# The walk of the sums of the complex products: channel innermost in place of frequency innermost

## The chip, the cores and the metric

The kernel runs on one core of one Trainium2 chip. The metric is the device time in microseconds (us) of one execution; a kernel's time is the median of its runs. Engines: PE is TensorE (PEld its weight loads), DVE is VectorE, ACT is ScalarE, POOL is GpSimd, SP is SyncE, which issues most of the transfers.

## The reference, cut to what matters

Two blocks follow each other on a sequence of S = 2048 rows and D = 640 channels: a long convolution that is gated, and a token-mixing network of two matrix products. The change lies in the long convolution:

```python
kv = k_shift * v                                   # short convolution of k, times v
kv_f = rfft(kv padded to 2 * S along the sequence)
kf_f = rfft(ssm_k padded to 2 * S)
y_f = kv_f * kf_f                                  # complex, per channel
y = irfft(y_f)[:S] + kv * ssm_D
x = x + ga * (h * y)                               # h: the normalized, modulated input
```

After it come a second normalization, `gelu(h @ w1 + b1) @ w2 + b2` along the sequence, a gate and the residual. A complex product is four real products and two sums: the real part is a difference, the imaginary part a sum. These two sums are what the change touches.

## The kernel before, in words

The channels go through the convolution in five blocks of 128 (`c` = 0 to 4; the texts call them blocks 0 to 4). A partition holds a position of the sequence or of the spectrum for half of the channels, and the transform is split in two steps of matmuls on PE in each direction:

- `step1(side, t)` (line 218) is the first step of the forward transform, for the data (`side` 0) and for the filter (`side` 1). ACT copies its result from PSUM to Z (line 220).
- `f2(g)` (line 234) is the second step, for group g of 8 frequencies, eight groups a block. Its result lies in PSUM, data and filter side by side. ACT copies the filter's part to `kt` (line 238). `mul` then makes the products on DVE, two instructions of 512 elements a partition, into one of two halves of the tile P (`pa` and `pb`, 512 words each). `add` makes the two sums from P into Y, 256 elements a partition each.
- `i2(r)` (line 263) is the first step back. It reads Y as the weights of its matmuls, all 64 frequencies of two channels at a time, so it needs the sums of all eight groups. ACT copies its result to `T2` in the tile of Z (line 271; in the last block half of it on DVE, line 269).
- `i1(half)` (line 282) is the second step back, into PSUM.
- `gate` multiplies by the normalized input on DVE and adds to the residual on POOL (the tiles xa and xb).

All elementwise operations of two tensors go through one helper, `TT`, and so all show line 59 in the profile; their tiles tell them apart: p is written by `mul`, y by `add`, tap, kt and x by the short convolution, aux by the gate and the modulation.

The order of work is written out by hand, each engine takes its instructions in that order, and the waits follow from the tiles. In the loop over the groups (`for g in range(8)`), the pass for g issues f2(g), the products of group g - 1, and the sums of group g - 2, and beside these, on ACT, two rows of the normalized input (line 289), and on DVE some operations of the next block's short convolution (`dv`). The sums go to POOL; only group 7's, in blocks 1 to 4, go to DVE (`pa_next(dve if c else pool)`). P has two halves, so the products of group g wait until the sums of group g - 2 have read them. After the loop PE takes two parts of the next block's `step1`, in blocks 1 to 3, and then `i2(0)`. In block 0 the modulation comes in between: SP loads the weights `w_mod` (line 335) and PE multiplies them (`mod_part`, line 342). `perm_add` is a small sum on POOL (one partition, 64 elements, in place with a step of 32 words) that adds `ssm_D` to the filter.

P and Y are laid out so: P holds for each of the 8 frequencies k, then for the two terms r, 32 channels i in a run; Y holds for real and imaginary part, for each of 32 channels, 64 frequencies in a run.

Of the kernel before, what the change touches and what calls it, by code (L numbers as in the profile page):

```python
# [49 lines left out]
def mixer_kernel(ctx: ExitStack, tc: tile.TileContext, q, k, v, shift_k, ssm_k, ssm_D, w1, b1, w2, b2, c,  # L50
# [8 lines left out]
    TT = lambda eng, o, a, b, op: eng.tensor_tensor(o, a, b, op=op)  # L59
    uid = [0]  # L60

    def mem(tag, n, name=None):

        return sb.tile([128, n], F32, name=name or tag, tag=tag, bufs=1)
# [4 lines left out]
    def psum(slot=None):  # L69

        uid[0] += 1
        slot = ring[uid[0] % len(ring)] if slot is None else slot
        return psp.tile([128, 1024], F32, name=f"pst_{uid[0]}", tag=f"pst{slot}", bufs=1)
# [23 lines left out]
    Y = T_y.rearrange("p (r i k) -> p r i k", r=2, i=32)  # L97
# [126 lines left out]
    def f2(g):  # L224

        ps = psum()
        for kk in range(8):
            k1 = 8 * g + kk
            for ri in range(2):
                for h in range(2):  # L230
                    o = 128 * kk + 64 * ri
                    rhs = bass.AP(tensor=T_z.tensor, offset=T_z.offset + 128 * h + 2 * k1,
                                  ap=[T_z.ap[0], [256, 32], [1, 2]])
                    pe.matmul(ps[64 * h:64 * h + 64, o:o + 64], W2[k1 // 32][:, 2 * (k1 % 32) + ri], rhs, start=True, stop=True)  # L234
        pv = ps.rearrange("p (m s i) -> p m s i", s=2, i=32)
        xs_ = pv[:, :, 0]
        kt = KT[g % 2]
        act.activation(kt.rearrange("p (m i) -> p m i", i=32), pv[:, :, 1], AF.Copy)  # L238
        pa, pb = P[:, 1024 * (g % 2):1024 * (g % 2) + 512], P[:, 1024 * (g % 2) + 512:1024 * (g % 2) + 1024]
        m16 = lambda t: t.rearrange("p (m i) -> p m i", i=32)  # L240

        def mul():
            TT(dve, m16(pa), xs_, m16(kt), ALU.mult)
            sw = bass.AP(tensor=kt.tensor, offset=kt.offset + 32, ap=[kt.ap[0], [64, 8], [-32, 2], [1, 32]])
            TT(dve, pb.rearrange("p (k r i) -> p k r i", k=8, r=2), xs_.rearrange("p (k r) i -> p k r i", r=2), sw,
               ALU.mult)

        def add(eng=pool):
            for ri, t, op in ((0, pa, ALU.subtract), (1, pb, ALU.add)):
                t = t.rearrange("p (k r i) -> p r i k", k=8, r=2)  # L250
                TT(eng, Y[:, ri, :, 8 * g:8 * g + 8], t[:, 0], t[:, 1], op)
        return mul, add


# [255 lines left out]
    for c in range(NC):  # L510
# [86 lines left out]
        else:  # L597
# [6 lines left out]
            t = mem("in", 4288, "wb3")  # L604
# [4 lines left out]
        if c:  # L609
            dv(7 if cn is not None else 8)  # L610
            i2(0)
            if cn is None:
                mod_part(tap, 3, pl[3])
                i2(1, dve)
                t = mem("y", 4096, "wb2")
# [390 lines left out]
    for s in range(NW):  # L1006
        i = NF + s
# [77 lines left out]
```

## Time and profile before

| | |
|---|---|
| median of 3 runs | 722.91 us (722.14 to 728.45) |
| span of the profiled execution | 727.4 us, granted clock 0.969 |
| PE busy | 656.2 us, 90% |
| DVE busy | 492.5 us, 68% |
| ACT busy | 297.3 us, 41% |
| POOL busy | 155.7 us, 21% |
| the sums on POOL | 72, 92.2 us in all |
| the sums on DVE | 8, 9.1 us in all |

The profile gives the span of the profiled execution, from its first instruction to its last, as its own time; it stands 4.5 us above the median of the runs. A row of a timeline or of the chain begins with the start in us from the span's start and the duration in us. A row that groups instructions ends with their total busy time in us, the mean of one in ns, and the idle time ahead of them on their engine with what ended it. `out<-in` are tile names; 128x512 is partitions by elements.

### The profile page before, as it was taken

The numbers are of one execution on the slowest core, as the hardware profiler recorded it, in microseconds if no ns is written. First come the engines' busy times: TensorE is split into PE (matmuls) and PEld (weight loads), VectorE is DVE, ScalarE is ACT, GpSimd is POOL, SyncE is SP. The second block draws the span as 40 slices with busy tenths as digits, with TensorE's granted clock in tenths as the row PEclk, the third lists the DMA queues.
The fourth block names the chain that finished last, engine by engine and source line by source line (L and its number), as shares of the span: only waits on it lengthen the run. The fifth ranks groups of instructions, "written<-read, shape, count | busy, mean of one in ns | idle before, by whom it ended". The sixth has DMA issues, their size and how long they took to land.

```text
span 727.4 us, 20779 instructions
## 1 busy us (share of the span) xinstructions
PE 656.2 (90%) x9131; PEld 632.1 (87%) x9131; DVE 492.5 (68%) x861; ACT 297.3 (41%) x465; POOL 155.7 (21%) x135
## 2 busy tenths in 40 slices
PE   0798868989999989987899999999999989999997
PEld 0798558988989989777799999999999989999997
DVE  7768458958879738678895312311299868888887
ACT  0533464535645645344776312311335222333222
POOL 5197029714725428100000000000000000000000
PEclk9999989989999999679999999999999999999999
DMA  9978988427243522333022353344163333455510
GB/s 184 242 223 221 388 147 169 112 45 166 45 80 87 169 54 69 110 88 88 10 50 58 62 113 60 59 93 81 50 188 102 116 104 117 149 156 174 150 53 37
DMA packets 167184, 84.90 MB, mean 117 GB/s; under 512 B 89235, under 2 KB 157622, under 8 KB 167094
## 3 DMA queue, kind: packets, MB, share of 16 engines
q1 hardware_dynamic: 162546, 82.27, 44.8%
q10 hardware_dynamic: 4548, 1.31, 1.0%
q8 instruction: 71, 1.16, 0.7%
q14 instruction: 19, 0.16, 0.1%
HBM read 73.07 MB, written 10.49 MB: 115 GB/s over the span
## 4 chain that ended last, share of the span: by engine, by line
PE 44%; DVE 24%; POOL 8%; SPq 7%; issue 6%; ACT 6%; DMA 5%; ACTq 0%; DVEq 0%; POOLq 0%
PE pst L432 21%; PE pst L1026 7%; POOL y L59 6%; PE pst L263 5%; DVE m_w L59 4%; PE pst L218 3%; SPq L495 3%; PE pst L282 3%; DVE m_x L59 3%; DVE tap L59 3%; PE pst L234 2%; ACT m_w L939 2%; DVE kt L59 2%; PE pst L951 2%; DMA in<-in_A_k_dram 2%
## 5 line engine op out<-in xcount | busy, mean ns | idle before, releaser
L234 PEld LDWEIGHTS pst<-z,w 128*64 128x64 f32 x2560 | 94.7, 141 | 7.7 <-ACT z L220 7.3
L234 PE MATMUL pst<-z,w 128*64 128x64 f32 x2560 | 95.7, 240 | 6.2 <-ACT z L220 6.1
L59 POOL TENSOR_TENSOR y<-p 128x256 f32<-128x256 f32 x72 | 92.2, 1340 | 22.3 <-DVE p L59 21.9
L59 DVE TENSOR_TENSOR p<-pst,kt 128x512 f32<-128x512 f32 x80 | 52.9, 689 | 24.8 <-ACT kt L238 14.3
L218 PE MATMUL pst<-v,x 128*64 128x128 f32 x640 | 46.3, 306 | 25.9 <-DVE x L59 25.9
L218 PEld LDWEIGHTS pst<-v,x 128*64 128x64 f32 x640 | 44.3, 221 | 26.5 <-POOL t L457 23.6
L220 ACT ACTIVATE z<-pst 128x1024 f32<-128x1024 f32 x40 | 45.8, 1146 | 52.1 <-PE pst L218 31.7
L263 PEld LDWEIGHTS pst<-v,y 32*128 32x128 f32 x1280 | 43.3, 210 | 6.7 <-POOL y L59 3.2
L263 PE MATMUL pst<-v,y 32*128 32x64 f32 x1280 | 45.4, 297 | 3.0 <-DVE y L59 2.1
L238 ACT ACTIVATE kt<-pst 128x512 f32<-128x512 f32 x40 | 25.1, 629 | 52.5 <-PE pst L234 30.2
L830 ACT ACTIVATE pst<-pst,sm 128x640 f32<-128x640 f32 x14 | 10.7, 767 | 85.9 <-PE pst L432 85.9
L951 PE MATMUL pst<-r_z,m_w 128*128 128x320 f32 x222 | 43.1, 313 | 3.0 <-DVE m_w L59 2.5
L218 PE MATMUL pst<-v,p 128*64 128x128 f32 x640 | 39.1, 281 | 4.8 <-DVE aux L59 3.2
L218 PEld LDWEIGHTS pst<-v,p 128*64 128x64 f32 x640 | 36.6, 141 | 6.0 <-DVE aux L59 3.5
L939 ACT ACTIVATE m_w<-m_v 128x896 fp32r<-128x896 f32 x24 | 22.1, 949 | 42.7 <-DVE m_v L59 31.0
L951 PEld LDWEIGHTS pst<-r_z,m_w 128*128 128x128 f32 x222 | 34.8, 188 | 5.0 <-DVE m_w L59 4.0
L59 DVE TENSOR_TENSOR tap<-tap,kt 128x512 f32<-128x512 f32 x51 | 35.6, 697 | 1.3
L59 DVE TENSOR_TENSOR kt<-in,tap 128x512 f32<-128x512 f32 x51 | 35.0, 686 | 1.4
L271 ACT ACTIVATE z<-pst 128x512 f32<-128x512 f32 x38 | 21.2, 656 | 29.9 <-PE pst L263 29.9
L59 DVE TENSOR_TENSOR m_w<-m_v,m_w 128x896 fp32r<-128x896 f32 x24 | 26.0, 1087 | 10.5 <-ACT m_w L939 10.5
L282 PEld LDWEIGHTS pst<-z,v 64*64 64x64 f32 x1280 | 25.5, 161 | 8.6 <-issue 5.0
L282 PE MATMUL pst<-z,v 64*64 64x64 f32 x1280 | 27.5, 248 | 5.9 <-issue 3.5
(277 smaller groups left out, 1417.6 us busy)
## 6 DMA issues: line engine op xcount, KB each, us to landing
x<-in_B_w_dram SPq DMA_DIRECT2D x22, 512.0 KB
m_v<-in_B_w_dram SPq DMA_DIRECT2D x15, 384.0 KB
x<-in_B_w_dram SPq DMA_DIRECT2D x14, 384.0 KB
aux<-in_A_ssm_k_dram SPq DMA_DIRECT2D x10, 512.0 KB
in<-in_A_k_dram SPq DMA_DIRECT2D x36, 128.0 KB
in<-in_A_v_dram SPq DMA_DIRECT2D x36, 128.0 KB
m_x<-xs SPq DMA_DIRECT2D x28, 160.0 KB
out_dram<-m_x SPq DMA_DIRECT2D x28, 160.0 KB
```

Source lines behind the costliest of these rows:

```text
L59: TT = lambda eng, o, a, b, op: eng.tensor_tensor(o, a, b, op=op)
L218: pe.matmul(ps[64 * ri:64 * ri + 64, o:o + 128], lhs, F1[:, 128 * ri:128 * ri + 128], start=True, stop=True)
L220: evac = lambda: act.activation(Z[:, side, t].rearrange("p a k e -> p e a k"), ps.rearrange("p (e a k) -> p e a k", a=8, e=2), AF.Copy)
L234: pe.matmul(ps[64 * h:64 * h + 64, o:o + 64], W2[k1 // 32][:, 2 * (k1 % 32) + ri], rhs, start=True, stop=True)
L238: act.activation(kt.rearrange("p (m i) -> p m i", i=32), pv[:, :, 1], AF.Copy)
L263: pe.matmul(pp[qd // 2][:, o:o + 64], Y[p, ri, i:i + 2].rearrange("p i k -> p (i k)"), V2[p, 64 * ri:64 * ri + 64], start=ri == 0, stop=ri ...
L282: pe.matmul(ps[64 * b:64 * b + 64, 512 * e + 64 * jj:512 * e + 64 * jj + 64], V1[p, ri, n2], T2[p, :, 32 * ri + n2], start=ri == 0, stop=r ...
L432: pe.matmul(ps[0:m, h, 0:320], w_.bitcast(F32R), r_[:, 320 * h:320 * h + 320].bitcast(F32R), start=first and i == 0, stop=last and i == 2)
L495: sync.dma_start(XH[j // 8][64 * b:64 * b + 64, j % 8], dram(q, (16 * b + j) * D, [[32 * D, 64], [1, D]]))
L939: act.activation(W[n][0].bitcast(F32R), a(w_), AF.Copy)
L951: pe.matmul(bank[n], w[:, i].bitcast(F32R), r.bitcast(F32R), start=i == 0 and k == 0, stop=i == 6 and k == 2)
L1026: pe.matmul(acc[s][:, h, 0:320], w[:, f_].bitcast(F32R), u[r + h].bitcast(F32R), start=f_ == 0 and k == 0, stop=f_ == NF - 1 and k == 2)
```

## The change

Both sums walk over the same elements of the same tiles and give the same result. Before, the innermost loop of the access pattern went over the 8 frequencies of the group, and the outer loop over the 32 channels: each operand was read with a step of 64 words, and the result was written in runs of 8 words. After, the innermost loop goes over the 32 channels, and the outer loop over the 8 frequencies: both operands are read in runs of 32 words, and the result is written with a step of 64 words.

```diff
         def add(eng=pool):
             for ri, t, op in ((0, pa, ALU.subtract), (1, pb, ALU.add)):
-                t = t.rearrange("p (k r i) -> p r i k", k=8, r=2)
-                TT(eng, Y[:, ri, :, 8 * g:8 * g + 8], t[:, 0], t[:, 1], op)
+                t = t.rearrange("p (k r i) -> p r k i", k=8, r=2)
+                TT(eng, Y[:, ri, :, 8 * g:8 * g + 8].rearrange("p i k -> p k i"), t[:, 0], t[:, 1], op)
         return mul, add
```

## The prediction

> **What bounds the kernel now.** I read the engine table and the slices of the page first.
>
> ```profile
> span 727.4 us, 20779 instructions
> ...
> PE 656.2 (90%) x9131; PEld 632.1 (87%) x9131; DVE 492.5 (68%) x861; ACT 297.3 (41%) x465; POOL 155.7 (21%) x135
> ...
> POOL 5197029714725428100000000000000000000000
> ...
> PE 44%; DVE 24%; POOL 8%; SPq 7%; issue 6%; ACT 6%; DMA 5%; ACTq 0%; DVEq 0%; POOLq 0%
> PE pst L432 21%; PE pst L1026 7%; POOL y L59 6%; PE pst L263 5%; DVE m_w L59 4%; PE pst L218 3%; SPq L495 3%; PE pst L282 3%; DVE m_x L59 3%; DVE tap L59 3%; PE pst L234 2%; ACT m_w L939 2%; DVE kt L59 2%; PE pst L951 2%; DMA in<-in_A_k_dram 2%
> ```
>
> TensorE is busy 90% of the span. POOL works only in the first 17 of the 40 slices, the convolution, and there the chain that ended last gives the changed sums ("POOL y L59") 6% of the whole span. That looks like 44 us to be had. It is not, and the next two views say why. The first gives the busy time of each engine in the spectral step of channel blocks 1 to 4; the second is the table of waits from 115 to 310 us.
>
> ```profile
> 116.00:140.00 24.00, 23.62 (x576) 23.14 (x576) 21.21 (x34) 13.22 (x27) 23.82 (x19) 1.00 0.71 157
> 171.00:195.00 24.00, 23.57 (x584) 23.31 (x584) 20.20 (x30) 13.73 (x28) 18.74 (x16) 1.00 0.45 105
> 221.60:245.70 24.10, 23.48 (x584) 23.22 (x584) 20.39 (x31) 13.34 (x26) 18.66 (x16) 1.00 0.42 137
> 271.50:294.20 22.70, 22.44 (x548) 20.32 (x548) 17.57 (x50) 13.67 (x34) 17.87 (x14) 1.00 0.33 92
> ```
>
> ```profile
> DVE p L59 <- POOL y L59: 6.4, 15, 0.7
> ...
> PEld pst L263 <- POOL y L59: 3.2, 4, 0.9
> ...
> PE pst L263 <- DVE y L59: 2.1, 3, 0.8
> ...
> PE pst L263 <- ACT wb L408: 0.2, 1, 0.2
> ```
>
> Columns of the first: window, its length, then busy PE, PEld, DVE, ACT, POOL, then granted clock, DMA share, GB/s. PE is busy 23.57 of 24.00 us while POOL is busy 18.74: both run almost through, so the chain can be drawn through POOL although PE would allow little less. What PE truly loses to the sums is in the waits: 2.1 us in three places (the sums that VectorE does last) and 0.2 us in a fourth, where the weight load also waits for POOL. How one such place comes about, in block 2: the chain of waits, PE's timeline, DVE's timeline, and ACT's.
>
> ```profile
> 181.99 10.21 POOL y L59 x8
> ...
> 192.23 0.69 DVE p L59
> ...
> 193.72 1.53 DVE y L59
> ...
> 195.38 3.58 PE pst L263 x120
> ```
>
> ```profile
> 189.71 0.55 PE L234 MATMUL pst<-z,w 128*64 128x64 f32 x10
> 190.08 4.31 PE L218 MATMUL pst<-v,x 128*64 128x128 f32 x64
> 194.32 0.45 PE L263 MATMUL pst<-v,y 32*128 32x64 f32 x8
> 195.38 3.58 PE L263 MATMUL pst<-v,y 32*128 32x64 f32 x120 [0.61 <-DVE y L59]
> ```
>
> ```profile
> 191.13 0.69 DVE L59 TENSOR_TENSOR p<-pst,kt 128x512 f32<-128x512 f32 x1 [0.39 <-POOL y L59]
> 192.23 0.69 DVE L59 TENSOR_TENSOR p<-pst,kt 128x512 f32<-128x512 f32 x1 [0.41 <-POOL y L59]
> 192.84 2.40 DVE L59 TENSOR_TENSOR y<-p 128x256 f32<-128x256 f32 x2
> ```
>
> ```profile
> 190.35 0.60 ACT L238 ACTIVATE kt<-pst 128x512 f32<-128x512 f32 x1 [0.96 <-ACT aux L289]
> ```
>
> POOL is behind, so each product of group 7 on DVE waits until POOL has read the half of P that it overwrites. The last product ends at 192.92; DVE then makes group 7's two sums itself, 2.40 us beside POOL's group 6, and ends at 195.24. PE covers most of that with 4.31 us of other matmuls, then waits 0.61 us.
>
> **The change, part by part.** Both sums of a group keep their engine, place, waits and sizes. No DMA, matmul, copy or wait is added or moved, and Y has the same layout after, so i2's weight loads cost the same. What changes is the walk: before, both operands step 64 words at each element and the result is written in runs of 8; after, both operands are read in runs of 32 and the result steps 64 words. So only the duration of 72 sums on POOL and 8 on DVE changes, and who waits for them.
>
> *Price on POOL.* The nearest rows (shortest/median/longest ns):
>
> ```profile
> L59 POOL TENSOR_TENSOR y<-p x72: 1071/1368/1827, 48.3 to 292.5; 128x256 f32<-128x256 f32 x72
> ...
> L59 POOL TENSOR_TENSOR t<-in,t x12: 1262/1272/2246, 8.6 to 112.4; 128x512 f32<-128x512 f32 x12
> ...
> L59 POOL TENSOR_TENSOR aux<-aux,rows x8: 344/356/627, 19.1 to 231.9; 1x64 f32<-1x64 f32 x8
> L59 POOL TENSOR_TENSOR xa<-xa,aux x4: 2377/2384/2472, 116.3 to 262.2; 128x1024 f32<-128x1024 f32 x4
> ```
>
> ```profile
> L59 POOL TENSOR_TENSOR y<-p 128x256 f32<-128x256 f32 x56 | 72.5, 1356 | 22.3 <-DVE p L59 21.9
> ```
>
> With long runs on all operands, 512 elements take 1262 ns and 1024 take 2377: 2.18 ns an element and 147 ns fixed. The old sum takes (1071 - 147)/256 = 3.61 ns: two stepped reads add 1.43, or 0.72 each. The small sum aux<-aux,rows (perm_add) has one stepped read, one run read and a stepped write, 32 words a step: (344 - 147)/64 = 3.08 ns, 0.90 over the run price. 0.72 of that is the read, if reads add; 0.18 is left for the stepped write. The new sum is then 147 + 256 x (2.18 + 0.18) = 751 ns undisturbed. Ends: a free write, 147 + 256 x 2.18 = 705 ns; a write that comes on top of the reads, at half of the two stepped reads' 3.61, 147 + 256 x (2.18 + 1.80) = 1166 ns. I take 751, since perm_add is the one row with a stepped write; its weakness is that it runs on one partition. In company the old sums averaged 1356 over blocks 1 to 4 (the last row, the window from 116 to 300 us), 1.27 times their shortest; the same factor gives 0.95 us, with ends of 0.90 and 1.48.
>
> *Price on DVE.*
>
> ```profile
> L59 DVE TENSOR_TENSOR y<-p x8: 597/1204/1515, 138.7 to 294.0; 128x256 f32<-128x256 f32 x8
> ```
>
> ```profile
> 290.41 3.19 POOL L59 TENSOR_TENSOR y<-p 128x256 f32<-128x256 f32 x3
> ...
> 291.46 1.29 DVE L59 TENSOR_TENSOR p<-pst,kt 128x512 f32<-128x512 f32 x2 [0.99 <-ACT kt L238]
> ...
> 292.67 1.96 DVE L59 TENSOR_TENSOR y<-p 128x256 f32<-128x256 f32 x2
> ```
>
> Alone the old sum takes 597 ns (the second one of block 4; POOL is done at 293.60); beside POOL's sums up to 1515. No row has a stepped result alone on DVE. Bounds: 597, as cheap as now, and 1515, as bad as now in company. I take 0.6, since POOL will be done by then.
>
> *What becomes of the wait.*
>
> ```profile
> L234 PE MATMUL pst<-z,w 128*64 128x64 f32 x2560 | 95.7, 240 | 6.2 <-ACT z L220 6.1
> ```
>
> Block 2 again, with sums of 0.95 us: POOL needs 1.9 us a group, under PE's pace (95.7 us of f2 matmuls, this row, over 40 groups: 2.4 us each). So group 7's products wait for their copy alone, which ends at 190.95; the pair takes 1.29 as in block 4, to about 192.3; the two sums 1.2, to 193.5. PE is free at 194.39. The wait of 0.61 is gone with 0.9 us to spare; even DVE sums of 2.40 for the pair would end at 194.7 and leave 0.3. What is last next is PE itself: the gain stops there however cheap the sum becomes.
>
> Sum: 2.1 us for blocks 1 to 3 and 0.2 for block 4 make 2.3 us. Up to 3.2 if the weight load's earlier start (3.2 in four places) counts whole. Of the 6.4 us that DVE waited for POOL only this reaches PE; the rest DVE has over.
>
> *Block 0* gives nothing. It has 16 sums on POOL, and i2 follows them, but the chain there goes elsewhere:
>
> ```profile
> 70.89 0.48 SPq L335
> ...
> 71.47 10.30 DMA aux<-in_w_mod_dram
> ...
> 81.82 2.01 PE tap L342 x12
> ...
> 116.28 2.47 POOL xa L59
> ...
> 118.75 2.12 POOL xb L59
> ```
>
> SP issues loads back to back up to the weights of the modulation, and PE waits for their landing at 81.8 us; whatever PE gains before 71 us is given back there. In block 1 POOL first has the output gate's two adds to do (the last two rows, 116.3 to 120.9 us) and starts late, but at 1.9 us a group against 2.4 it makes up 0.5 us a group and has seven groups for it.
>
> Against the profiled span: 727.4 - 2.3 = 725.1. That execution is 4.5 us above the median of the runs, 722.91, and near the longest, 728.45; nothing in the steps scales with that, so I take the same 2.3 us off the median: **720.6 us**.
>
> **Rivals.**
> 1. *The walk makes no difference*: a step of 64 words costs a result what it costs two operands, and the sum stays at 1.36 us. Then 722.9. For it: the trace has no full-width stepped write. Against it: perm_add leaves 0.18 ns of its 0.90 for a stepped write. The Trainium skill speaks for this rival: Vector Engine (DVE) Microarchitecture Reference, "Measured stream behaviour on trn2", has a result that hops at every element at about the price of both sources hopping, 1.71 and 1.76 ns a column. By that rule DVE's 597 would not move, and if POOL obeyed it the sum of my terms would be nil; that is measured on VectorE, and no row here shows a stepped result by itself.
> 2. *Slower: the stepped write is not hidden behind the reads.* The sum becomes 1.48 us. The place is the one above: each block's 14 POOL sums already end too late for i2, so what they grow by is PE's wait. 56 x (1.48 - 1.36) = 6.7 us: 729.6. It is slower from 1.36 us a sum on, and by 1% from 1.36 + 7.2/56 = 1.49. For it: the end is worked out from this trace. Against it: perm_add would then take 147 + 64 x (2.18 + 0.72 + 1.80) = 448 ns and takes 344.
> 3. *Slower by much: stepped writes collide with DVE's own writes* as stepped sums on both engines did here, 597 to 1515, 2.5 times. The sum becomes 751 x 2.5 = 1.9 us and blocks 1 to 4 grow by 56 x 0.54 = 30 us: 753. Against it: DVE's products write in runs, not in steps.
> 4. *Faster by over 1%* would need 7.2 us; PE waits for the sums 3.2 us at the most. Only if block 0's earlier end shifted the loads would it come, and SP's chain excludes that.
>
> **How the numbers follow.** A measurement of this kernel tells about 1% from no change. Forecast (sums below 1.3 us, 719 to 722): 0.58. Rival 1: 0.11. Rival 2: 0.18, half of it beyond 1%. Rival 3: 0.11. Rival 4: 0.02, and 0.01 of the forecast's own spread with it. So faster 0.03, same 0.77, slower 0.20. The range: low is the forecast with 3.2 us and 2 us of scatter between medians, 718; high is rival 2's price, cut to 729 so that 2 in 10 stay out, nearly all above.
>
> **What would show it.** The sums on POOL near 0.75 us at their shortest and under 1.2 in the mean; "PE pst L263 <- DVE y" and "PEld pst L263 <- POOL y" gone from the waits; DVE's products of group 7 released by ACT's copy and no longer by POOL; POOL y gone from the chain; PE's matmuls of block 2 just as long. I am wrong in the price if the sums' mean is over 1.36 us, and wrong in the cover if they are short and PE still waits ahead of L263, or if more than 3 us come off.

## The result, and the profile after

| | before | after |
|---|---|---|
| median of the runs | 722.54 us (722.14 to 728.45, 4 runs) | 716.92 us (712.14 to 718.91, 4 runs) |
| ratio of the runs | 1 | 0.9887 (0.9841 to 0.9932) |
| span of the profiled execution | 727.4 us | 716.8 us |
| granted clock, mean over that execution | 0.969 | 0.985 |

The changed kernel is faster by 1.1%, 0.7 to 1.6% by the interval. The two medians are 5.6 us apart. With the executions of the experiments, 106 of the kernel before have a mean of 723.5 us and a mean clock of 0.975, and 16 of the changed one 716.3 us and 0.981: 7.2 us. The means leave out executions that lie more than 1.5% above the fastest of their kernel, such as those that the traces of `e3_wait` (735.6 us) and of the kernel with all stepped (732.5 us) show. The two profiled executions are 10.6 us apart, more than either figure, since the one before was a long one.

The page of the changed kernel, its engine table and the chain that ended last:

```profile
span 716.8 us, 20779 instructions
...
PE 646.4 (90%) x9131; PEld 624.4 (87%) x9131; DVE 487.0 (68%) x861; ACT 296.9 (41%) x465; POOL 118.4 (17%) x135
...
PE 54%; DVE 22%; DMA 8%; ACT 5%; SPq 5%; issue 4%; POOL 0%; ACTq 0%; DVEq 0%
PE pst L432 21%; PE pst L234 9%; PE pst L218 8%; PE pst L1026 7%; PE pst L263 4%; DVE m_w L59 4%; SPq L495 3%; DVE m_x L59 3%; PE pst L282 2%; DMA aux<-in_A_ssm_k_dram 2%; ACT m_w L939 2%; PE pst L951 2%; DMA aux<-in_w_mod_dram 2%; DVE m_x L960 1%; DVE m_v L59 1%
```

POOL had 8% of the chain and has 0%; the matmuls of the spectral step (L234) have its place, with 9%. The sums, on POOL and on DVE (shortest/median/longest ns), and those on POOL from 116 to 300 us (the third row, whose last numbers before the idle time are total us and mean ns):

```profile
L59 POOL TENSOR_TENSOR y<-p x72: 729/772/1549, 48.7 to 285.9; 128x256 f32<-128x256 f32 x72
```

```profile
L59 DVE TENSOR_TENSOR y<-p x8: 603/619/641, 139.3 to 288.4; 128x256 f32<-128x256 f32 x8
```

```profile
L59 POOL TENSOR_TENSOR y<-p 128x256 f32<-128x256 f32 x56 | 43.0, 803 | 41.1 <-DVE p L59 40.9
```

PE, DVE and ACT around i2 of block 2, in three timelines:

```profile
187.45 4.22 PE L218 MATMUL pst<-v,x 128*64 128x128 f32 x63
191.60 3.80 PE L263 MATMUL pst<-v,y 32*128 32x64 f32 x128
```

```profile
188.42 1.29 DVE L59 TENSOR_TENSOR p<-pst,kt 128x512 f32<-128x512 f32 x2 [1.01 <-POOL y L59]
189.62 1.06 DVE L59 TENSOR_TENSOR y<-p 128x256 f32<-128x256 f32 x2
```

```profile
187.71 0.60 ACT L238 ACTIVATE kt<-pst 128x512 f32<-128x512 f32 x1 [0.93 <-ACT aux L289]
```

The products of group 7 start at 188.42, right after their copy (188.31), and the two sums end at 190.68; PE comes from other work at 191.67 and goes on without a wait. (The row names POOL as the releaser; POOL's sums had ended at 188.33, 20 ns after the copy, so both were done together.) The groups of i2's matmuls on the two pages, before and then after, show it for all blocks:

```profile
L263 PE MATMUL pst<-v,y 32*128 32x64 f32 x1280 | 45.4, 297 | 3.0 <-DVE y L59 2.1
```

```profile
L263 PE MATMUL pst<-v,y 32*128 32x64 f32 x1280 | 39.2, 272 | 0.6 <-ACT z L220 0.6
```

The idle time ahead of i2 fell from 3.0 to 0.6 us; what is left belongs to block 0. That is the 2.3 us that the prediction spoke of. But the same 1280 matmuls also became shorter, 45.4 to 39.2 us, though Y did not change. The granted clock (the column after the five engines) says why, before and after:

```profile
140.00:143.50 3.50, 2.71 (x90) 2.58 (x90) 3.40 (x5) 3.15 (x2) 0.64 (x1) 1.00 0.11 36
143.70:150.50 6.80, 6.80 (x99) 6.35 (x92) 6.66 (x6) 3.27 (x5) 0.00 (x0) 0.50 0.00 0
...
290.00:297.20 7.20, 6.90 (x151) 4.69 (x146) 6.21 (x10) 4.48 (x9) 3.60 (x4) 1.00 0.62 175
297.30:314.30 17.00, 15.47 (x313) 13.02 (x311) 8.70 (x12) 4.34 (x8) 0.00 (x0) 0.50 0.11 44
```

```profile
141.00:151.00 10.00, 10.00 (x294) 9.69 (x291) 8.64 (x8) 6.41 (x7) 0.00 (x0) 1.00 0.04 12
...
239.00:249.00 10.00, 10.00 (x287) 9.69 (x284) 6.22 (x11) 6.51 (x8) 0.00 (x0) 1.00 0.46 100
289.00:299.00 10.00, 9.06 (x271) 7.85 (x268) 9.13 (x12) 4.74 (x10) 0.00 (x0) 1.00 0.44 153
299.70:303.00 3.30, 3.30 (x128) 3.30 (x127) 1.22 (x2) 0.41 (x1) 0.00 (x0) 0.50 0.02 5
```

Before, PE waited ahead of i2 in block 1 at 140.5 to 141.3 us, and from 143.7 on it had half clock for 6.8 us; from 297.3, inside i2 of block 4, it had half clock for 17 us. After, i2 of blocks 1 to 4 runs at full clock, and the first stretch at half clock in this part begins at 299.7 and lasts 3.3 us. Both traces have more such stretches in block 0 and behind the convolution. Each execution has them at its own places, so two traces prove nothing; the experiments had to.

### The profile page after: what moved, and what is told of

Its sections match the earlier page's. It is cut to its first block, busy times and chain, and to the rows that moved or that the text cites. A ratio compares the mean times of both kernels' runs of the same rounds, so it can differ in the third digit from the quotient of the medians.

```text
span 716.8 us, 20779 instructions
## 1 busy us (share of the span) xinstructions
PE 646.4 (90%) x9131; PEld 624.4 (87%) x9131; DVE 487.0 (68%) x861; ACT 296.9 (41%) x465; POOL 118.4 (17%) x135
## 4 chain that ended last, share of the span: by engine, by line
PE 54%; DVE 22%; DMA 8%; ACT 5%; SPq 5%; issue 4%; POOL 0%; ACTq 0%; DVEq 0%
PE pst L432 21%; PE pst L234 9%; PE pst L218 8%; PE pst L1026 7%; PE pst L263 4%; DVE m_w L59 4%; SPq L495 3%; DVE m_x L59 3%; PE pst L282 2%; DMA aux<-in_A_ssm_k_dram 2%; ACT m_w L939 2%; PE pst L951 2%; DMA aux<-in_w_mod_dram 2%; DVE m_x L960 1%; DVE m_v L59 1%
## 5 line engine op out<-in xcount | busy, mean ns | idle before, releaser
L234 PEld LDWEIGHTS pst<-z,w 128*64 128x64 f32 x2560 | 94.7, 141 | 7.7 <-ACT z L220 7.3
L234 PE MATMUL pst<-z,w 128*64 128x64 f32 x2560 | 95.7, 240 | 6.2 <-ACT z L220 6.1
L218 PE MATMUL pst<-v,x 128*64 128x128 f32 x640 | 44.8, 298 | 24.1 <-DVE x L59 24.0
L59 DVE TENSOR_TENSOR p<-pst,kt 128x512 f32<-128x512 f32 x80 | 51.4, 685 | 21.2 <-ACT kt L238 13.4
L218 PEld LDWEIGHTS pst<-v,x 128*64 128x64 f32 x640 | 42.8, 221 | 24.8 <-POOL t L457 23.4
L59 POOL TENSOR_TENSOR y<-p 128x256 f32<-128x256 f32 x72 | 55.2, 800 | 43.4 <-DVE p L59 43.3
L263 PEld LDWEIGHTS pst<-v,y 32*128 32x128 f32 x1280 | 37.7, 187 | 3.1 <-issue 1.6
L263 PE MATMUL pst<-v,y 32*128 32x64 f32 x1280 | 39.2, 272 | 0.6 <-ACT z L220 0.6
L939 ACT ACTIVATE m_w<-m_p 128x896 fp32r<-128x896 f32 x12 | 11.4, 952 | 47.1 <-DVE m_p L59 40.7
```

The costliest lines, as they stand in the source:

```text
L218: pe.matmul(ps[64 * ri:64 * ri + 64, o:o + 128], lhs, F1[:, 128 * ri:128 * ri + 128], start=True, stop=True)
L263: pe.matmul(pp[qd // 2][:, o:o + 64], Y[p, ri, i:i + 2].rearrange("p i k -> p (i k)"), V2[p, 64 * ri:64 * ri + 64], start=ri == 0, stop=ri ...
L939: act.activation(W[n][0].bitcast(F32R), a(w_), AF.Copy)
```

## The experiments

All times are means over executions, with the standard error; the clock is the mean granted clock of the same executions. "Waits" are PE's waits for the sums ahead of i2 that the kernel's trace shows; in the last row but one it is what the waits ahead of f2 grew by.

| kernel | time, us | clock | waits, us | sums on POOL, shortest ns |
|---|---|---|---|---|
| before | 723.5 +- 0.3 (106) | 0.975 | 2.1 to 2.4 | 1071 |
| after | 716.3 +- 0.5 (16) | 0.981 | 0 | 729 |
| new walk on POOL alone | 719.4 +- 0.7 (12) | 0.979 | 0 | 725 |
| new walk on DVE alone | 722.7 +- 0.7 (12) | 0.976 | 1.1 | 1057 |
| no step at all | 717.7 +- 0.6 (12) | 0.980 | 0 | 723 |
| all stepped | 722.9 +- 0.9 (9) | 0.977 | 1.8 | 1067 |
| after, POOL made late by runs | 735.8 +- 1.4 (6) | 0.960 | 5.5 | |
| after, one late sum a block | 728.9 +- 1.3 (9) | 0.968 | 6.1 | |
| before, 8 useless matmuls | 723.7 +- 0.9 (12) | 0.977 | 0 | 1050 |
| before, 3 useless matmuls | 722.3 +- 0.7 (12) | 0.976 | 0 | |
| before, other matmuls ahead of i2 | 727.8 +- 1.1 (10) | 0.963 | see below | |
| after, other matmuls ahead of i2 | 725.5 +- 0.8 (12) | 0.963 | see below | |
| after, longer wait ahead of f2 | 722.6 +- 0.6 (12) | 0.976 | 4.5 (f2) | |
| after, a wait of i1 filled | 715.5 +- 0.7 (6) | 0.981 | 0 | |

**Both kernels again.**

> The kernel before once more, to see how far its executions scatter and what clock they are granted. Two theories of the 5.6 us between the medians, where the prediction allowed 2.3 to 3.2. Cover: only PE's waits ahead of i2 went (2.3 us), and the rest is scatter of the executions and of the granted clock, which has nothing to do with the change; then the executions here scatter over 5 us or more, and before and after overlap. Clock: each wait of PE ahead of i2 is followed by half clock, and the change takes both away; then the executions before all show a lower mean clock (near 0.97) than those after (near 0.985), and half clock stands behind the waits in this trace too.

> The changed kernel once more. Cover: 2 to 3 us under before, scatter as large as before's. Clock: 5 to 7 us under before, mean clock near 0.985 in every execution, no half clock between the starts of the spectral steps of blocks 1 and 4.

> The changed kernel once more beside the next two, on their chip. From 10 executions so far: mean 716.0, mean clock 0.981; before, from 105: mean 724.2, clock 0.974. Expected: 716 to 718, clock 0.979 to 0.982, and no wait ahead of i2.

Before against itself: ratio 0.9972 (0.9928 to 1.0016), 716.0 to 730.7 us. After: 0.9884 (0.9838 to 0.9929), 713.3 to 717.8; and on another chip 0.9890 (0.9846 to 0.9933), 715.1 to 718.4. Cover was right that executions scatter, by 15 us, and wrong that the rest is scatter: three comparisons agree on 1.1%. Clock was right in part. The changed kernel's mean clock is the higher one, 0.979 and 0.982 in the two rows against 0.976 and 0.973 for the kernel before beside them, and i2 of blocks 1 to 4 has no half clock in either trace. But the clocks of single executions overlap (0.974 to 0.985 in these two rows), and in `e1_before` itself the clock is 0.978, with a time 6.5 us above that of `e1_after`: there the mean clock does not carry the gain. And the trace of `e1_before` shows waits ahead of i2 (2.4 us) and full clock in i2 of blocks 1 to 4. So a wait brings half clock in some executions and not in each. Over the 106 executions of the kernel before, the time falls by 4.4 us for 0.01 of clock (a straight line through them). The difference of 0.0064 in clock is then worth 2.8 us, and 4.4 us are left at equal clock. The line is rough: fitted the other way, the clock over the time, it gives 7.4 us for 0.01, and 4.7 us for the difference.

The granted clock of the traces says where it happens. Take the time from the first f2 of block 1 to the last i2 of block 4. Six traces in which PE does not wait for sums ahead of i2, and nothing else was done to PE there, have no stretch at half clock that begins in it: three of the changed kernel, the new walk on POOL alone, no step, and the one with a wait of i1 filled. Of the six traces with such waits four have some, 24 us in all (`before`), 34 us (all stepped), 34 us (POOL made late by runs) and 31 us (one late sum a block); `e1_before` and the new walk on DVE alone have none.

**Half of the change each.** In `add`, the new patterns only if `eng is pool`, or only if `eng is dve`.

> The new walk for the 72 sums on POOL, the old one for DVE's 8. If POOL's lateness is all of it: the whole gain of the changed kernel within 1 us, since DVE's two sums alone take 2 x 0.6 in either walk once POOL is done ahead of them. If DVE's own sums matter: at least 1 us of the gain stays away.

> The old walk on POOL, the new one for DVE's 8 sums. POOL stays late: its last sums end where they ended, PE waits for them instead. If POOL's lateness is all of it: within 1 us of before. If the collision of stepped reads of both engines is what made the wait: DVE's pair falls from 2.4 to about 1.3 us and half of the gain or more is there.

POOL alone: 0.9956 (0.9922 to 0.9989); DVE alone: 0.9973 (0.9938 to 1.0009). DVE alone is not told from before; its pair beside the late POOL still takes 0.94 and 1.48 us, so the pair is slow because POOL's sums run beside it, and not because of its own reads. POOL alone removes all waits ahead of i2, as the whole change does, and ends 3.1 us above it; less than the whole gain, against my expectation. Its DVE pair takes 1.2 us in place of 1.1 and is done 0.9 us before PE needs it. Its trace shows no place in blocks 1 to 4 where it loses to the changed kernel. Its clock, lower by 0.002, is worth 1.0 us by the line above. The rest stays open.

**The price of a step.** The elements are paired otherwise in these two, so the values of Y are others; sizes, tiles and waits are the same. No step at all:

```diff
-                t = t.rearrange("p (k r i) -> p r k i", k=8, r=2)
-                TT(eng, Y[:, ri, :, 8 * g:8 * g + 8].rearrange("p i k -> p k i"), t[:, 0], t[:, 1], op)
+                t = t.rearrange("p (k r j l) -> p r k j l", k=8, r=2, j=4)
+                y = Y[:, ri, :, 8 * g:8 * g + 8].rearrange("p (a b) k -> p a b k", a=8)
+                TT(eng, y, t[:, 0], t[:, 1], op)
```

> Both operands read in runs of 8 and the result written in runs of 8; the elements are paired otherwise, so the output is another one. This gives the price of the sum without any step. By my terms 705 ns undisturbed, about 0.73 in company. Lateness: since PE does not wait for the sums any more, the time stays at that of the changed kernel, within 1.5 us. Rival, every saved part of a sum counts: 1 us or more faster than the changed kernel.

```profile
L59 POOL TENSOR_TENSOR y<-p x72: 723/764/800, 48.9 to 283.7; 128x256 f32<-128x256 f32 x72
L59 DVE TENSOR_TENSOR y<-p x8: 416/418/422, 137.2 to 286.1; 128x256 f32<-128x256 f32 x8
```

All stepped (`"p (k r j l) -> p r j l k"` read, `"p (b l) k -> p k b l"` written):

> Both operands read with a step of 64 words as before and the result written with a step of 64 words too; the elements are paired otherwise, so the output is another one. If a stepped write hides behind the reads: 1.07 us undisturbed as before, and the time of before within 2 us. If it comes on top: 1.4 us or more, and POOL's 14 sums a block end 5 us later in each of blocks 1 to 4: 15 us or more over before.

```profile
L59 POOL TENSOR_TENSOR y<-p x72: 1067/1364/1834, 49.0 to 295.2; 128x256 f32<-128x256 f32 x72
L59 DVE TENSOR_TENSOR y<-p x8: 621/1264/1592, 139.7 to 296.8; 128x256 f32<-128x256 f32 x8
```

On POOL the step of the result costs 6 ns beside reads in runs (723 to 729) and nothing beside stepped reads (1071 and 1067); the two stepped reads cost 348 beside a result in runs and 338 beside a stepped one. On DVE a sum takes 416 ns in runs, 597 with stepped reads, 603 with a stepped result and 621 with both: there either side costs about the same, and only once. The time of the kernel without steps, 0.9942 (0.9912 to 0.9972), is not below the changed one's; that of the kernel with all stepped is before's, 1.0008 (0.9966 to 1.0049). DVE's sums, cheaper by a third without steps (416 for 603), buy nothing more once PE no longer waits; POOL's are hardly cheaper there and tell nothing on that. The Trainium skill's Vector Engine (DVE) Microarchitecture Reference ("Measured stream behaviour on trn2") gives VectorE this: a result that hops costs about what two hopping sources cost, and the two add only partly. DVE's four rows agree (181, 187 and 205 ns over the sum without steps); POOL's do not follow it (348, 6 and 344).

**Late again.** In the changed kernel, each POOL sum made once more over 5 of its 8 frequencies:

```diff
                 TT(eng, y, t[:, 0], t[:, 1], op)
+                if eng is pool:
+                    TT(eng, y[:, 0:5], t[:, 0, 0:5], t[:, 1, 0:5], op)
```

> The changed kernel, but on POOL each sum is followed by the same sum once more over 5 of its 8 frequencies, so that POOL needs about as long a group as before (0.77 + 0.50 = 1.27 us against 1.36) and reads in runs all the same. Theory lateness: what the change gave is that POOL is done in time, and the granted clock follows from PE's waits; then PE waits ahead of i2 again, 0.4 to 0.8 us in each of blocks 1 to 4, the mean clock falls back to about 0.975 and at least 5 of the 8 us are lost. Rival, collision: stepped reads on POOL took time from others, DVE above all; then at least half of the gain stays although POOL is late.

1.0200 (1.0149 to 1.0252): slower than before by 12 us. POOL needs 1.39 us for a sum and its repetition, 1.34 for a sum before. Collision of stepped reads as the cause of the gain falls: with every read in runs, the gain is gone. But the loss is more than PE's waits, 5.5 us, and the clock is the lowest of all, 0.960. In block 2 PE waited ahead of i2, and then:

```profile
196.83 3.48 PE L266 MATMUL pst<-v,y 32*128 32x64 f32 x104 [1.09 <-POOL y L59]
```

```profile
195.00:199.00 4.00, 2.62 (x84) 2.48 (x88) 3.86 (x6) 3.01 (x2) 1.70 (x3) 1.00 0.03 8
199.20:216.20 17.00, 17.00 (x266) 16.10 (x265) 6.57 (x6) 6.20 (x10) 0.00 (x0) 0.51 0.39 64
```

17 us at half clock, though PE never stood still in them. To have nothing but the wait, the next kernel makes only group 6's last sum again, 4 times (in blocks 2 and 3 once more, and a half):

```diff
+            if eng is pool and g == 6 and c:
+                for k in (8, 8, 8, 8) + ((8, 4) if c in (2, 3) else ()):
+                    TT(eng, y[:, 0:k], t[:, 0, 0:k], t[:, 1, 0:k], op)
```

> The changed kernel, quick sums and all; only group 6's second sum on POOL is made again 4 to 6 times in blocks 1 to 4, so that it lands about when it landed in the kernel before (22.9 to 24.9 us after the start of the spectral step). PE's wait ahead of i2 is back, and nothing else of the old kernel. Theory lateness with clock: PE waits 0.3 to 0.9 us in each of the four blocks, the mean clock falls from 0.981 to about 0.975, and the whole gain is lost, 722 to 725 us. Rival, lateness alone: only the 2 to 3 us of the waits are lost, 718 to 720, the clock stays. Rival, collision of stepped reads: 716 to 718.

1.0067 (1.0025 to 1.0109): 12.6 us above the changed kernel, the gain lost and more. The waits came out longer than I meant, 6.1 us in its trace, 3.1 of them in block 3, with half clock behind:

```profile
PE pst L267 <- POOL y L59: 6.1, 4, 3.1
```

```profile
249.98 2.42 PE L267 MATMUL pst<-v,y 32*128 32x64 f32 x72 [3.09 <-POOL y L59]
```

```profile
252.00:258.70 6.70, 6.70 (x92) 6.25 (x90) 0.65 (x4) 2.37 (x6) 0.00 (x0) 0.50 0.70 157
```

The clock fell to 0.968 in the mean. Both rivals fall, lateness alone too: the waits themselves are half of what is lost.

**A wait elsewhere.** In the changed kernel, the last copy ahead of f2 made twice:

```diff
-        for t in range(1 if c else 0, 4):
+        for t in range(1 if c else 0, 3):
             step1(1, t)
+        copy = step1(1, 3, True)
+        copy()
+        copy()
```

> The changed kernel with PE made to wait at another place: ACT makes the last copy ahead of the spectral step twice, so that PE's wait there, 1.24 us in each of blocks 1 to 4, grows by about 1.1 us. If any wait of PE costs clock: clock 0.972 or less and 8 us or more lost, as where PE waited ahead of i2. If a wait costs clock only inside i2, where the matmuls use 32 rows: 4.5 us lost, the waits themselves, clock near 0.980.

0.9965 (0.9935 to 0.9996). PE's waits ahead of f2 grew from 6.1 to 10.6 us, 2.4 in each of blocks 1 to 4, and 6.3 us were lost, clock 0.976. Neither expectation holds: the clock is paid here too, but 4.5 us of waiting cost 1.4 times themselves, against 2.1 times ahead of i2 (12.6 for 6.1, with the waits of one trace each). Its trace has a stretch at half clock behind one of these waits:

```profile
PE pst L234 <- ACT z L220: 10.6, 5, 2.4
```

```profile
218.09 1.70 PE L234 MATMUL pst<-z,w 128*64 128x64 f32 x31 [2.36 <-ACT z L220]
```

```profile
219.20:222.50 3.30, 3.30 (x71) 3.30 (x69) 1.93 (x4) 0.94 (x3) 0.00 (x0) 0.57 0.00 0
```

3.3 us long, where those behind i2 are 6.8 to 17.

**Filling the wait.** In the kernel before, 8 or 3 useless matmuls ahead of i2 (`pe.matmul(pp[0][:, 0:64], F1[:, 0:128], F1[:, 0:64], ...)`):

> The kernel before with 8 small matmuls of no use (0.6 us) ahead of i2's first part in blocks 1 to 4, so that PE works where it waited; POOL is as late as before. Clock theory: it is PE's standing still that costs clock; the mean clock rises from 0.975 toward 0.981 and the time falls 2 to 4 us under before. Cover theory: the clock stays, the time is that of before within 1 us.

> The kernel before with 3 useless matmuls ahead of i2 in place of 8, about as long as the wait (0.7 us), in blocks 1 to 4. At full clock nothing is won or lost. Clock: mean clock up by 0.003 or more over before and 1.5 to 3 us faster. Otherwise: before, within 1 us.

1.0025 (0.9988 to 1.0062) and 0.9969 (0.9939 to 0.9998). The 8 took PE 1.9 us and not 0.6, so i2 began later than before; that this cost nothing in the mean speaks for a gain in clock (0.977), and is no proof. Its trace has one stretch of 6.8 us at half clock, in i2 of block 3, right behind a wait of 1.1 us for which it shows no releaser. The 3 fitted: no wait ahead of i2, no delay over before, clock 0.976; 1.2 us gained, or 1.8 and 0.002 of clock against the executions of before that ran beside them (724.2 us, 0.974). That is at or under the lower edge of the 1.5 to 3 us expected, and the clock rose by less than 0.003. If PE's standing still were all that costs clock, only the delay of the sums, some 2 us, would part this kernel from the changed one; it is 6.0 us above it. So filling the wait does not give back what the change gives. In the changed kernel, 6 of them in another wait, ahead of the last block's i1:

> The changed kernel with 6 useless matmuls (1.5 us) in the wait of 1.48 us ahead of the last block's first i1, behind which the trace has a stretch of 3.4 us at half clock at 300 us. If PE's standing still there brings the half clock: that stretch is gone and 1 to 2 us with it. Otherwise: the changed kernel within 1 us.

0.9868 (0.9820 to 0.9917), 0.8 us below the changed kernel, less than the errors; the stretch at 300 us is gone from its trace. Not decided. It is the fastest mean of all, and not a version that I can call faster.

**Other work in front.** `step1(0, 2)`, which stood between i2(0) and i2(1), moved ahead of i2(0) in blocks 1 to 3, in the kernel before and in the changed one:

```diff
+            if cn is not None:
+                step1(0, 2)
             i2(0)
...
             run(po)
-            step1(0, 2)
             i2(1)
```

> The kernel before, slow sums and all; only 32 matmuls that PE has to do anyway (the third part of the next block's first step, 2.3 us) stand ahead of i2(0) in blocks 1 to 3 and no longer behind it. PE then has work while the sums are late. Lateness with clock: no wait ahead of i2 in blocks 1 to 3, clock near 0.979, 4 to 6 us under before. Lateness alone: 2 us under before, clock as before. Collision: no gain.

> The changed kernel with the same 32 matmuls ahead of i2(0). Since PE does not wait there any more, every theory gives the time of the changed kernel within 1.5 us; a loss would say that the moved matmuls delay i2 and what follows it.

1.0036 (0.9997 to 1.0076) and 1.0022 (0.9985 to 1.0058). Both expectations fell, the second by 9 us. The waits for sums are gone in blocks 1 to 3, but i2(0) and i2(1) now stand back to back, and the second waits for ACT to empty PSUM (block 2 of the first of the two):

```profile
205.45 2.96 PE L263 MATMUL pst<-v,y 32*128 32x64 f32 x66 [1.02 <-ACT z L271]
```

```profile
207.00:217.00 10.00, 10.00 (x192) 9.55 (x192) 3.55 (x4) 3.33 (x5) 0.00 (x0) 0.51 0.24 38
```

One wait of 1.0 us a block inside i2 brought about 10 us of half clock in blocks 1 and 2 of both traces, and 6.7 in block 3: clock 0.963, and 9 us. Two things changed at once here, i2's parts back to back and a wait inside them. My reading is that a wait inside i2 is the dearer the less i2 is mixed with other matmuls; that the long run of i2 alone brings the half clock was not separated from it.

## Why the prediction was right or wrong

- *The walk and its price: right.* 751 ns were predicted for a sum on POOL undisturbed, 729 measured; 0.95 us in company, 0.80 measured (1.10 times the shortest, not 1.27). The write is hidden (6 ns, 0.02 an element where perm_add had given 0.18), so rival 2 falls, and rival 1 with it on POOL; on DVE its rule held (597 and 603). Rival 3 falls: DVE's sums take 603 to 641 ns and DVE's products their 0.69 us. DVE's sum was predicted at 0.6.
- *What becomes of the wait: right.* POOL left the chain; the group's products start with their copy, though POOL was done only 20 ns after it; DVE's sums end 22.2 us after the start of block 2's spectral step, predicted 22.3; PE does not wait.
- *Block 0: right.* PE reaches the modulation earlier and waits there until the weights land: 82.46 us after, 81.82 before.
- *The sum: wrong.* The prediction had 2.3 us, 3.2 at the most, and 720.6; the median is 716.9, 5.6 us under before's, and the means are 7.2 us apart. The step that failed is "What is last next is PE itself: the gain stops there however cheap the sum becomes". PE's pace was taken as given, and it is not: the granted clock fell where waits ahead of i2 were put in, and such a wait is paid twice, as itself and in clock. The traces show both parts. From the first matmul of f2 in block 1 to that in block 4 PE takes 149.2, 149.7 and 149.4 us in the three of the changed kernel, 151.7 in `e1_before`, with the waits and no half clock, and 155.4 in `before`, with the waits and 6.8 us of half clock: 2.3 us for the waits, near the 2.1 predicted for these three, and 3.7 more that were in no term. In the mean the clock's part is not known as well. Of the 7.2 us between the means, 2.3 are the waits, and 2.8 to 4.7 go with the clock by the two ways to draw the line; at the 2.1 times that `e3_wait` paid, waits of 2.1 to 2.4 us make 4.4 to 5.0 in all. Between nothing and some 2 us, with an error of 0.6, are explained by neither.
- The prediction saw the sign of it and passed by: it noted that the profiled execution stood 4.5 us above the median, and held that "nothing in the steps scales with that". The clock by slices on the page before pointed there: 0.6 and 0.7 in slices 17 and 18, 291 to 327 us, from i2 of block 4 on.

```profile
PEclk9999989989999999679999999999999999999999
```

- Its rival 4, faster by over 1%, was dismissed since "PE waits for the sums 3.2 us at the most". That bound holds for the waits, not for the time.
- *Open:* what the granted clock counts. Waits lower it, more inside i2 than ahead of f2; useless matmuls in the wait gave back 0.001 to 0.002 of its 0.006, and 1 to 2 us of 7; i2's parts back to back make it worse. Whether PE's idle time or the small use of the array in i2 (32 rows) is what is counted was not separated. Open too is why the new walk on POOL alone stays 3 us behind.

## What to carry to other kernels

On GpSimd choose the walk of a two-operand operation by its reads: in these sums of 128x256 elements a step in the result was free, a step in both operands cost half as much again. Where PE is nearly always busy, price a wait of PE not at its length but at that and the clock behind it, and read the granted clock just behind each wait before calling PE's pace fixed. With a scatter of 15 us between executions of one kernel, a single pair of profiles tells where, not how much.

## What the runs showed of the hardware that was not expected

- Stretches at half clock came behind waits of PE of about 1 us, in some executions and not in each (0.8 us ahead of the 6.8 us at 143.7 in the kernel before; 1.0 us ahead of the 10 us at 207 in the moved one). The Trainium skill, TensorE: Matmul & The Clock Gate ("Part 1: The HAM clock gate"), has the array at half rate by default and after an idle window of about 3.4 us, and activity as what releases it. The lengths here agree (3.3, 6.8, 10 and 17 us, near one, two, three and five such windows); that the half rate comes after an idle window of that length does not, since the waits ahead of i2's stretches shown above were 0.8, 1.0, 1.1 and 3.1 us. There the measurement decides.
- Stepped sums on two engines at once hurt both: DVE 597 to 1515 ns in the kernel before, POOL 1071 to 1.5 us. With POOL reading in runs, DVE's stepped sum beside a late POOL still took 589 to 901 ns in one kernel (POOL made late by runs) and 598 to 1126 in another (one late sum a block). So part of it is the other engine's sum, whatever its reads.
- DVE and POOL differ in what a step costs: DVE 416, 597, 603 and 621 ns (none, reads, result, both), POOL 723, 1071, 729 and 1067.
